# Second layer of the last six groups as seven block products, growth with 40 weight columns, decays turned ahead of minus x

## The chip, the cores and the metric

One core of one Trainium2 chip. The metric is device time in microseconds (us) of one execution of the whole program, the median of several runs; lower is better. The engines are TensorE (PE in the profile; its weight loads are listed apart as PEld), VectorE (DVE), ScalarE (ACT), GpSimd (POOL) and SyncE (SP), which issues most of the DMAs.

## What is computed

A recurrent attention layer, then a feed-forward layer on its output, all in float32:

```python
# r, k, v, w, a, b: (B=4, H=8, S=768, D=40); state: (B, H, D, D), zero at first
for t in range(S):
    y[t]  = einsum('bhd,bhde->bhe', r[t], state)
    Sa    = einsum('bhde,bhe->bhd', state, a[t])
    state = state * w[t][:, :, None, :] - outer(Sa, b[t]) + outer(v[t], k[t])
x = y.transpose(0, 2, 1, 3).reshape(3072, 320)
out = relu(x @ w_in) ** 2 @ w_out        # w_in: 320 x 2048, w_out: 2048 x 320
```

## The kernel before, in words

**Chunks and groups.** The sequence is cut into chunks of 128 tokens: 6 chunks of each of 4 batches, 24 in all, in the order chunk 0 of all batches, chunk 1 of all batches, and so on. Within a chunk the recurrence becomes matrix products and the solution of a triangular system. Two chunks that follow each other make a group (12 groups), the unit of the feed-forward layer.

**A chunk's work** is a chain (`chain`, lines 632 to 717) with a stop after each stage: right side `x_` from state and A, two products with the inverse T (`times_t`, giving `minus_x`), transposes of minus x (line 671), the products with `rT` masked to RX, then `y_`, and *growth*: the products that add to the state (lines 688 to 692), for each of 8 heads k by v and b by minus x. Growth exists for chunks 0 to 19, since the last chunk of a batch leaves no state behind. Its outputs lie two heads to a column of partitions, the even head at partition 0, the odd one at 64; a head has 40 columns, but weights were loaded 64 wide, 24 of them zero.

**Ahead of the chain** of the next chunk stand its turned inputs: `turn_rv` (transposes of r and v, copied by ACT at lines 560, 561), `make_rv` (RV), `turn_k` (transposes of k, DVE line 548), `turn_down` (line 582: transposes of the decays, whose result stays in PSUM), `scale_kb` (DVE line 588 reads that result), `make_a`, `turn_state` (line 598). `early` does the first part of chunks far ahead (scans of w, N) and is spent by slot 14. GpSimd solves the triangular systems (lines 478, 480), unit by unit of up to 4 chunks, and `inverses` loads the solved T (line 507).

**Order.** An opening, written out word by word, takes chunks 0 to 6. Then slot i (`sorted_slot`) finishes chunk i and turns chunk i + 1; its calls are the order of the instructions on each engine. `tick` after each step issues stores that were put off.

**The feed-forward layer** (`Ffn`). The first layer works by quads: 4 of the 16 blocks of 128 hidden features for a group's 256 tokens (`thirds` and `whole`), through two banks of PSUM (`ps_f`; in the tail, `ps_w`), ReLU by ACT (line 762) into `hidden`, squared by DVE (line 769). `hidden` holds six quads of 256 tokens, a ring. The second layer works by quarters (`make_quarter`): for one chunk, 4 matmuls whose weights are 128 hidden features by 128 tokens and whose moving side is 320 columns of `w_out`; four quarters fill a bank of `ps_f`, ACT copies it (line 790) and SP stores it. A slot begins two quarters (with `turn_rv` between them) and ends with two more; it makes two quads between. The group g has its quads in slots 2g + 3 and 2g + 4; its second layer begins at the end of slot 2g + 4. After slot 23 `rest` goes on with a quad and up to four quarters a turn (the tail).

Each float32 matmul of this kernel is two records in the profile, with a weight load each; a transpose is one.

Of the kernel before, what the change touches and what calls it, by code (L numbers as in the profile page):

```python
# [11 lines left out]
Alu = mybir.AluOpType  # L12
# [5 lines left out]
def kernel(  # L18
# [22 lines left out]
    nc = tc.nc  # L41
    ctx.enter_context(tc.manual_schedule())
    B, H, S, D = r.shape
# [42 lines left out]
    def mm(o, l_, r_, start):  # L86
        nc.tensor.matmul(o, l_, r_, start=start, stop=True, skip_group_check=True)  # L87
# [518 lines left out]
    def rest(i, g):  # L606
        begin(i, g)
        yield
        yield
        turn_k(i, g)  # L610
        yield
        make_a(i, g)
        yield
        turn_rv(i, g)
        yield
        make_rv(i, g)
        yield
        turn_down(i, g)
        yield
        scale_kb(i, g)  # L620
        yield
        yield
# [9 lines left out]
    def chain(i, g):  # L632
# [55 lines left out]
        if c < NCH - 1:  # L688
            grown = psum(ps_w)[:, :NP * D].rearrange("p (q d) -> p q d", q=NP)
            for l_, r_ in ((k_, v_), (b_, xn)):  # L690
                for h in range(H):
                    mm(grown[h % 2 * DP:(h % 2 + 1) * DP, h // 2], l_[:, h, :], r_[:, h, :D], l_ is k_ and h < 2)
        n = i % GB
        if n == 0:
            tokens[i // GB] = new("tokens", [128, NP, GB * C], 2)
# [1 line left out]
        nc.vector.tensor_tensor(t_, y_, g["up"][:, :, :C], Alu.mult)  # L697
        if c < NCH - 1:
            for e in range(2):
                rows = slice(e * DP, (e + 1) * DP)  # L700
                nc.vector.tensor_tensor(st[rows, :, e, :D], grown[rows], st[rows, :, e, :D], Alu.add)
            ended[bb] = new(f"end{bb}", [128, NP], 1)
            nc.scalar.copy(ended[bb], g["up"][:, :, C])
# [20 lines left out]
    class Ffn:  # L724
# [47 lines left out]

        def make_quarter(self):
            n, p = divmod(self.quarter, NQ)
            k = (n // GB) * NQ + p
            if n >= len(order) or self.squared <= k or left():
                return False
            if p == 0:
                self.out = psum(ps_f)[:, :DM]
            cols = slice((n % GB) * C, (n % GB + 1) * C)  # L780
            h_ = hidden[:, self.place(k)].rearrange("p e (f t) -> p e f t", f=2)
            for e in range(2):
                for m_ in range(2):
                    f = p * QF + 2 * m_ + e
                    mm(self.out, h_[:, e, m_, cols], w_out[:, f], p == 0 and e == 0 and m_ == 0)
            self.quarter += 1
            if p == NQ - 1:
                bb, c = order[n]
                o_ = new("o", [128, DM], 1)
                nc.scalar.copy(o_, self.out)  # L790
                at = bb * S + c * C
                store(out[at:at + C, :], o_, 6 if opening[0] else 2)
            return True

        def rest(self):
            self.tail = True
            last = len(order) * NQ
            while self.quarter < last:
                flush()
                self.thirds()  # L800
                self.whole()
                for _ in range(NQ):
                    self.make_quarter()
                self.square()


    second = Ffn()

# [175 lines left out]
    def sorted_slot(i, g, ch):  # L984
# [21 lines left out]
        fetch_next(j + 1, "r")  # L1006
        step(second.make_quarter)
        step(on(ch), of(decay_state))
        step(of(make_rv), second.thirds)
        step(on(ch), on(one))  # L1010
        if fine:
# [1 line left out]
        step(second.whole)  # L1013
        step(on(ch))
        step(on(one), of(turn_k))
        step(on(one), on(ch), of(turn_down))
        step(on(ch), of(scale_kb))
        if fine:
            join()
        step(on(ch), of(make_a), second.thirds, on(one))  # L1020
        fetch_next(j + 1, "v")
        step(of(turn_state), second.square, second.whole, on(two))
        if not early_join and not fine:
            join()
        run(ch)
# [54 lines left out]
```

## Time and profile before

| | |
|---|---|
| median of 3 runs | 950.41 us |
| the three runs | 949.51, 963.28, 950.41 us |
| span of the profiled execution | 949.3 us |
| mean granted TensorE clock | 0.958 |
| matmuls `ps_f<-w_out,hid` (second layer) | 768 records, 436 ns mean |
| matmuls `ps_f<-tokens,w_in` (first layer) | 672 records, 387 ns mean |
| growth, `ps_w<-in_v,in_k` and `ps_w<-minus_x,in_b` | 320 records each, 229 and 230 ns mean |

The profile is of one execution. Its page gives busy time by engine; tables by stretch give the same for parts of the span, with the granted clock; groups put together instructions of one line, engine and pair of tiles (`out<-in`), with count, busy time, mean length, and the idle time ahead of them with what ended it. The timeline shows runs of equal instructions: start, length, engine, line, count. Shown lengths of matmuls overlap, so that the distance from one start to the next says what one costs.

### The profile page before, as it was taken

The numbers are of one execution on the slowest core, as the hardware profiler recorded it, in microseconds if no ns is written. First come the engines' busy times: TensorE is split into PE (matmuls) and PEld (weight loads), VectorE is DVE, ScalarE is ACT, GpSimd is POOL, SyncE is SP. The second block draws the span as 40 slices with busy tenths as digits, with TensorE's granted clock in tenths as the row PEclk, the third lists the DMA queues.
The fourth block names the chain that finished last, engine by engine and source line by source line (L and its number), as shares of the span: only waits on it lengthen the run. The fifth ranks groups of instructions, "written<-read, shape, count | busy, mean of one in ns | idle before, by whom it ended". The sixth has DMA issues, their size and how long they took to land.

```text
span 949.3 us, 22557 instructions
## 1 busy us (share of the span) xinstructions
PE 896.9 (94%) x9116; PEld 719.2 (76%) x9116; DVE 462.1 (49%) x1131; ACT 284.8 (30%) x735; POOL 509.4 (54%) x935
## 2 busy tenths in 40 slices
PE   6578989879999999999999999999999999999998
PEld 4365656758787887888887888888888877887775
DVE  5927548788863355652664455544334331331110
ACT  3033334534532342342342232222221222222111
POOL 4568246064008786318999959999858870000000
PEclk9768988589999999999999999999999999999999
DMA  9788779856868477896846765604484154210000
GB/s 112 124 160 150 163 127 189 193 127 136 173 104 170 85 139 140 168 173 119 137 78 104 122 173 100 121 13 82 91 168 77 24 108 80 44 30 10 12 14 15
DMA packets 253266, 103.37 MB, mean 109 GB/s; under 512 B 234154, under 2 KB 240298, under 8 KB 252010
## 3 DMA queue, kind: packets, MB, share of 16 engines
q1 hardware_dynamic: 244709, 83.00, 49.2%
q0 software_dynamic: 3760, 17.10, 7.5%
q10 hardware_dynamic: 4693, 1.83, 0.9%
q8 instruction: 72, 1.18, 0.6%
q14 instruction: 32, 0.26, 0.1%
HBM read 69.00 MB, written 30.92 MB: 105 GB/s over the span
## 4 chain that ended last, share of the span: by engine, by line
PE 82%; DVE 6%; DMA 3%; ACT 3%; issue 2%; POOL 1%; SPq 1%; ACTq 0%; DVEq 0%; POOLq 0%
PE ps_f L87 40%; PE ps_w L87 17%; PE ps_c L87 14%; PE ps_w L331 5%; PE ps_f L264 2%; PE ps_c L671 2%; PE ps_c L598 1%; PE ps_w L582 1%; SPq L513 1%; DMA kept_q<-N 1%; DMA in_r<-in_r_dram 1%; DMA half_n<-kept_q 1%; ACT N L401 1%; DVE decay L381 1%; DVE decay L380 1%
## 5 line engine op out<-in xcount | busy, mean ns | idle before, releaser
L478 POOL TENSOR_TENSOR half_p<-half_n,half_t 128x462 f32<-128x462 f32 (+39 forms) x406 | 221.9, 547 | 74.3 <-DMA half_n<-kept_q 23.4
L480 POOL TENSOR_TENSOR half_t<-half_t,half_p 128x462 f32<-128x462 f32 (+39 forms) x406 | 237.7, 585 | 31.8
L87 PE MATMUL ps_f<-w_out,hid 128*128 128x320 f32 x768 | 218.4, 436 | 0.0
L87 PEld LDWEIGHTS ps_f<-w_out,hid 128*128 128x128 f32 x768 | 142.1, 190 | 54.0 <-issue 0.2
L87 PE MATMUL ps_f<-tokens,w_in 128*128 128x256 f32 x672 | 156.7, 387 | 0.0
L87 PEld LDWEIGHTS ps_f<-tokens,w_in 128*128 128x128 f32 x672 | 125.8, 192 | 18.7 <-issue 1.9
L769 DVE TENSOR_TENSOR hid<-hid 128x512 f32<-128x512 f32 x96 | 78.2, 853 | 50.6 <-ACT hid L762 50.2
L762 ACT ACTIVATE hid<-ps_f 128x512 f32<-128x512 f32 x84 | 49.5, 595 | 77.2 <-PE ps_f L87 77.1
L451 POOL DMA_DIRECT2D half_n<-kept_q x18 | 9.4, 526 | 88.4 <-DMA kept_m<-N 43.1
L372 DVE TENSOR_TENSOR_SCAN decay<-ps_w,ones 128x64 f32<-128x64 f32 x88 | 23.7, 270 | 67.0 <-PE ps_w L331 66.9
L697 DVE TENSOR_TENSOR tokens<-ps_c,dec 128x512 f32<-128x512 f32 x24 | 16.6, 691 | 79.6 <-PE ps_c L87 77.5
L347 DVE TENSOR_TENSOR RX<-ps_w,upper 128x512 f32<-128x512 f32 x48 | 30.8, 684 | 47.6 <-PE ps_w L87 47.4
L264 PE MATMUL ps_f<-ident 128*128 128x512 f32 (+3 forms) x108 | 49.8, 595 | 0.0
L347 DVE TENSOR_TENSOR RV<-ps_w,upper 128x512 f32<-128x512 f32 x48 | 30.9, 684 | 38.5 <-PE ps_w L87 38.2
L398 ACT COPY N<-ps_w 128x256 f32<-128x256 f32 x48 | 17.7, 368 | 94.4 <-PE ps_w L87 69.5
L87 PE MATMUL ps_f<-tokens,w_third 64*128 64x256 f32 x336 | 45.5, 381 | 0.1
L548 DVE TENSOR_TENSOR kvT<-ps_w,dec 128x512 f32<-128x512 f32 x24 | 16.4, 683 | 59.4 <-ACT minus_x L658 35.4
L87 PEld LDWEIGHTS ps_c<-xr,T 64*64 64x64 f32 x768 | 28.9, 143 | 20.7 <-issue 14.5
L570 DVE TENSOR_TENSOR f<-end,dec 128x4 f32<-128x4 f32 x20 | 7.5, 374 | 72.6 <-DMA dec<-kept_e 72.6
L331 PE MATMUL ps_w<-ident,in_ab 128*128 128x128 f32 x184 | 28.1, 298 | 11.9 <-DVE RV L347 10.0
L87 PE MATMUL ps_c<-xr,T 64*64 64x40 f32 x768 | 34.9, 237 | 3.8 <-ACT xr L647 2.6
L560 ACT COPY rT<-ps_w 128x512 f32<-128x512 f32 x24 | 14.0, 585 | 80.5 <-PE ps_w L331 80.4
(151 smaller groups left out, 1450.6 us busy)
## 6 DMA issues: line engine op xcount, KB each, us to landing
dec<-kept_e SPq DMA_DIRECT2D x22, 633.8 KB
kept_e<-decay SPq DMA_DIRECT2D x19, 633.8 KB
in_w<-in_w_dram SPq DMA_DIRECT2D x24, 160.0 KB
in_b<-in_b_dram SPq DMA_DIRECT2D x24, 160.0 KB
in_ab<-in_a_dram SPq DMA_DIRECT2D x24, 160.0 KB
in_r<-in_r_dram SPq DMA_DIRECT2D x24, 160.0 KB
in_v<-in_v_dram SPq DMA_DIRECT2D x24, 160.0 KB
out_dram<-o SPq DMA_DIRECT2D x24, 160.0 KB
```

Source lines behind the costliest of these rows:

```text
L87: nc.tensor.matmul(o, l_, r_, start=start, stop=True, skip_group_check=True)
L264: nc.tensor.matmul(fill_bank[:, :n * 128], ident, ident.unsqueeze(1).to_broadcast([128, n, 128]), start=True, stop=True, skip_group_check= ...
L331: nc.tensor.transpose(p_[:, q * 128:(q + 1) * 128], pair(x_, q), ident)
L347: nc.vector.tensor_tensor(t_, p_, over4(upper), Alu.mult)
L372: nc.vector.tensor_tensor_scan(up[:, q, MID + 1:C + 1], wT[:, q, MID:], ones, 1.0, Alu.mult, Alu.mult)
L398: nc.scalar.copy(plain, p_[:, ::2].rearrange("s h (f t) -> s f h t", f=2))
L478: eng.tensor_tensor(p_, part[:, at:at + m_].unsqueeze(1).to_broadcast([128, n, m_]), t3[:, :n, s:s + 1].to_broadcast([128, n, m_]), Alu.mult)
L480: eng.tensor_tensor(t3[:, :n, s + 1:], t3[:, :n, s + 1:], p_, Alu.subtract)
L671: nc.tensor.transpose(p_[:, q * 128:(q + 1) * 128], pair(xn, q), ident)
L697: nc.vector.tensor_tensor(t_, y_, g["up"][:, :, :C], Alu.mult)
L762: nc.scalar.activation(h_, p_.rearrange("p f t -> p (f t)"), Act.Relu)
L769: nc.vector.tensor_tensor(h_, h_, h_, Alu.mult)
```

## The change

The second layer of the groups 6 to 11 (`SEVEN = 6`) is no longer 32 matmuls of 320 columns but a 2 x 2 block product (two chunks by two halves of the hidden features, times two halves of the features by two halves of 160 output columns) in seven block products (Strassen's, in Winograd's form). Each of the seven has 8 matmuls of 128 x 128 weights and 160 moving columns. Sums ahead of and behind them are made by DVE:

- once, in slots 15 and 16 (`sum_weights`): three sums of blocks of `w_out` in tiles that are free by then, and one in place
- for each group, four sums of 128 x 1024 elements over the squared hidden features, in place
- for each group, eight sums of 128 x 160 elements, out of PSUM into two output tiles, and two ACT copies; both chunks are stored at the end

The pieces take the place of quarters, one for one; a group has eight places and seven pieces, so the eighth does nothing. The first piece, P4, needs all four quads of the group squared (in the last group P1 goes first, which needs two).

```diff
-                    mm(grown[h % 2 * DP:(h % 2 + 1) * DP, h // 2], l_[:, h, :], r_[:, h, :D], l_ is k_ and h < 2)
+                    mm(grown[h % 2 * DP:h % 2 * DP + D, h // 2], l_[:, h, :D], r_[:, h, :D], l_ is k_ and h < 2)
...
-                rows = slice(e * DP, (e + 1) * DP)
+                rows = slice(e * DP, e * DP + D)
                 nc.vector.tensor_tensor(st[rows, :, e, :D], grown[rows], st[rows, :, e, :D], Alu.add)
...
         def make_quarter(self):
             n, p = divmod(self.quarter, NQ)
+            if n < len(order) and n // GB >= SEVEN:
+                return self.make_piece(n // GB, n % GB * NQ + p)
...
+        def make_piece(self, g, at):
+            names = "P1 P4 P2 P7 P6 P5 P3" if g == len(order) // GB - 1 else "P4 P1 P2 P7 P6 P5 P3"
+            if at == 7:
+                self.quarter += 1
+                return True
+            name = names.split()[at]
+            if self.squared <= g * NQ + (1 if name == "P1" else 3):
+                return False
...
+            half, chunk = {"P1": (0, 0), "P2": (1, 0), "P4": (1, 1), "P7": (0, 1), "P6": (0, 0), "P5": (1, 1), "P3": (1, 0)}[name]
+            part = {"P1": 0, "P2": 2, "P4": 1, "P7": 0, "P6": 0, "P5": 1, "P3": 2}[name]
+            if at in (0, 3, 4):
+                self.bank = psum(ps_f)
...
+            for n in range(NF // 2):
+                k, e, m_ = n // 4, n // 2 % 2, n % 2
+                mm(ps[part], x_[:, n], seven[name][k * QF + 2 * m_ + e], at in (0, 3, 4) and n == 0)
...
+            a = lambda i, j: block(j, i)
...
+            if at == 1:
+                plus(a(1, 1), a(1, 0), a(1, 1))
+                less(a(1, 0), a(0, 0), a(1, 0))
+                less(a(0, 0), a(1, 1), a(0, 0))
+            if at == 2:
+                nc.scalar.copy(hi0, ps[0])
+                nc.scalar.copy(lo1, ps[1])
+                plus(lo0, ps[2], hi0)
+                less(a(0, 1), a(0, 1), a(0, 0))
+            if at == 3:
+                plus(hi1, ps[0], hi0)
+            if at == 6:
+                plus(hi0, ps[2], hi0)
+                plus(hi1, ps[0], hi1)
+                plus(hi0, ps[0], hi0)
+                less(lo1, hi1, lo1)
+                plus(hi0, ps[1], hi0)
+                plus(hi1, ps[1], hi1)
+                for n, o_ in enumerate(self.ends):
...
+                    store(out[row:row + C, :], o_, 2)
...
         step(on(ch), of(decay_state))
+        if i == 2 * SEVEN + 3:
+            sum_weights(0)
+        if i == 2 * SEVEN + 4:
+            sum_weights(3)
...
         step(on(one), of(turn_k))
-        step(on(one), on(ch), of(turn_down))
+        if i == 2 * SEVEN + 3:
+            sum_weights(1)
+        step(of(turn_down))
+        step(on(one), on(ch))
...
         step(of(turn_state), second.square, second.whole, on(two))
+        if i == 2 * SEVEN + 3:
+            sum_weights(2)
```

## The prediction on record

> **What bounds the kernel now.** I read the page first, then a table of stretches, then the groups by form, then the timeline of a late slot and of the end. The page:
>
> ```profile
> span 949.3 us, 22557 instructions
> ...
> PE 896.9 (94%) x9116; PEld 719.2 (76%) x9116; DVE 462.1 (49%) x1131; ACT 284.8 (30%) x735; POOL 509.4 (54%) x935
> ```
>
> A share of 94% over everything says little of a stage, so the stretches:
>
> ```profile
> core 0: us, PE busy (x) PEld busy (x) DVE busy (x) ACT busy (x) POOL busy (x), PEclk, DMA share, GB/s
> 0.00:100.00 100.00, 69.68 (x586) 50.52 (x587) 63.18 (x218) 29.40 (x80) 63.72 (x184) 0.81 0.84 138
> ...
> 330.00:545.00 215.00, 213.76 (x2537) 178.59 (x2536) 110.81 (x280) 73.11 (x202) 157.09 (x238) 1.00 0.75 131
> 545.00:640.00 95.00, 95.00 (x1009) 79.87 (x1008) 47.72 (x97) 25.87 (x67) 79.22 (x93) 1.00 0.51 103
> 640.00:735.00 95.00, 95.00 (x971) 77.59 (x970) 37.63 (x60) 21.88 (x51) 77.41 (x119) 1.00 0.55 104
> 735.00:830.00 95.00, 95.00 (x939) 77.41 (x939) 28.75 (x50) 23.70 (x54) 38.75 (x70) 1.00 0.32 63
> ```
>
> From 330 us on TensorE matmul is busy all the time at granted clock 1.00. All of the new second layer lies behind 640 us, where DVE has over half of its time free. So there the sum is one of matmul time, and other engines count only if they make TensorE wait.
>
> **The second layer.** How far apart matmuls start is what counts, since their shown durations overlap. Rows of the timeline (start, length, engine, line, instruction, count):
>
> ```profile
> 746.99 0.97 PEld L87 LDWEIGHTS ps_c<-rT,sd 128*128 128x128 f32 x8
> 747.10 1.06 PE L87 MATMUL ps_c<-rT,sd 128*128 128x128 f32 x8
> ...
> 751.43 3.62 PE L87 MATMUL ps_f<-tokens,w_in 128*128 128x256 f32 x16
> ...
> 932.53 13.08 PE L87 MATMUL ps_f<-w_out,hid 128*128 128x320 f32 x48
> ```
>
> and the groups by form (count, busy us, mean ns):
>
> ```profile
> L87 PE MATMUL ps_f<-w_out,hid 128*128 128x320 f32 x768 | 218.4, 436 | 0.0
> L87 PE MATMUL ps_f<-tokens,w_in 128*128 128x256 f32 x672 | 156.7, 387 | 0.0
> ...
> L87 PE MATMUL ps_c<-rT,sd 128*128 128x128 f32 x160 | 21.2, 276 | 0.0
> ...
> L87 PEld LDWEIGHTS ps_f<-w_out,hid 128*128 128x128 f32 x768 | 142.1, 190 | 54.0 <-issue 0.2
> ```
>
> 24 chunks by 16 products of 320 columns give 384 matmuls and 768 records, so each matmul is two records with a load each. Taking one duration off a run and dividing by the steps: 320 columns start every (13.08-0.44)/47 = 0.269 us, 256 every (3.62-0.39)/15 = 0.215, 128 every (1.06-0.28)/7 = 0.112. That is 0.84 ns a column within a few ns, also at 128 columns, where each matmul again has its own load of 128 columns (the row of PEld, as many as matmuls). A 160-column matmul is not in the trace; bounds from the neighbours are 0.112 and 0.215, and the straight line between them at 160 gives 0.138, the 320-column rate 0.135. I take 0.136.
>
> One group of two chunks now has 64 records, 64 x 0.269 = 17.2 us. The seven products are 7 x 8 matmuls of 160 columns, 112 records, 112 x 0.136 = 15.2 us. Six groups: **-11.9 us**. (One eighth of the columns is saved; the loads go from 64 to 112.)
>
> A rule that speaks against this stands in the Trainium skill, "TensorE: Matmul & The Clock Gate", The mechanism: a weight load runs beside matmuls in flight only if it goes to another group of rows. All loads here take all 128 rows; by that rule's letter 48 more loads of 0.112 us a group, 5.4, stand against 2.0 saved, +20 us over six groups instead of -11.9. The rows above disagree (269 ns from start to start with a 190 ns load for each). What is left of it is the first rival.
>
> **What the sums wait for.** DVE rows, with PSUM or SBUF sources, and the order of the work at the end of a slot:
>
> ```profile
> 756.77 0.61 PE L87 MATMUL ps_w<-in_v,in_k 128*64 128x40 f32 x16
> ...
> 756.99 0.69 DVE L697 TENSOR_TENSOR tokens<-ps_c,dec 128x512 f32<-128x512 f32 x1 [3.60 <-PE ps_c L87]
> ...
> 757.21 0.64 PE L87 MATMUL ps_w<-minus_x,in_b 128*64 128x40 f32 x16
> ...
> 757.68 0.75 PE L87 MATMUL ps_c<-state,dec 128*64 128x80 f32 x16
> ...
> 757.90 0.66 DVE L701 TENSOR_TENSOR state<-ps_w,state 64x160 f32<-64x160 f32 x2 [0.22 <-PE ps_w L87]
> ...
> 758.59 1.75 DVE L769 TENSOR_TENSOR hid<-hid 128x512 f32<-128x512 f32 x2
> ...
> 759.27 6.73 PE L87 MATMUL ps_f<-w_out,hid 128*128 128x320 f32 x24
> ```
>
> 512 elements take 0.69 us, 160 take 0.33, so an element is about 1.03 ns on 0.16 us: a block sum of 1024 is 1.22 us, 1.6 where GpSimd runs beside it (the 1.75 for two), and a weight sum of 1280 is 1.5 to 1.9. P4 comes first and needs the last square, which ends at 760.34. Its first six matmuls need only what was squared earlier or the first half, and at 759.27 they last 6 x 0.272 = 1.63 us, to 760.90; with growth 0.27 shorter still 0.3 us behind the square. The block sums start when P4 ends; the second, which P7 needs, is done 3.2 us later, and P1, P2 and the transposes of r and v lie between, 5.2 us. So **0** there, with 0.3 us of cover at P4; if DVE were late by 1 us, each of six groups would lose 0.7. In all the sums add 4 x 1.6 + 8 x 0.33 = 9 us of DVE in a group's two slots; of the 95 us from 640 on, some three slots, DVE has 57 free.
>
> Three things are not covered. The weight sums are made once, in slot 15: the second (1.9 us) goes between kT and the scaling of k and b, whose PSUM bank the second product of A takes over: **+1.1**. The others fall where DVE waits for a transfer or a product. Then the empty eighth piece: now a quarter lies between the transposes of r, v and the first product of T, and covers ACT's two copies.
>
> ```profile
> 765.84 0.60 PE L331 MATMUL ps_w<-ident,in_r 128*128 128x128 f32 x4
> ...
> 766.27 0.60 PE L331 MATMUL ps_w<-ident,in_v 128*128 128x128 f32 x4
> ...
> 766.47 0.59 ACT L560 COPY rT<-ps_w 128x512 f32<-128x512 f32 x1 [6.60 <-PE ps_w L331]
> ...
> 766.71 2.32 PE L87 MATMUL ps_f<-w_out,hid 128*128 128x320 f32 x8
> ...
> 766.96 0.59 ACT L561 COPY kvT<-ps_w 128x512 f32<-128x512 f32 x1
> ...
> 768.96 0.54 PEld L87 LDWEIGHTS ps_c<-xr,T 64*64 64x64 f32 x16 [0.44 <-issue]
> ...
> 769.55 1.16 PE L87 MATMUL ps_w<-rT,kvT 40*128 40x128 f32 x16
> ```
>
> kvT is there 1.71 us after the transposes begin. Without the quarter the product of T runs from 0.87 to 1.46, and rT,kvT would wait 0.3: in slots 18, 20 and 22 **+0.9**. Third, the end:
>
> ```profile
> 933.36 0.69 DVE L769 TENSOR_TENSOR hid<-hid 128x512 f32<-128x512 f32 x1 [1.03 <-ACT hid L762]
> ...
> 945.69 0.43 ACT L790 COPY o<-ps_f 128x320 f32<-128x320 f32 x1 [8.19 <-PE ps_f L87]
> ```
>
> After the last matmul stands one copy of 0.43 and a store to 949.3. Now come six sums of 0.33, 1.98, and two stores of 160 KB, the first one sum earlier: +1.55, and 0.15 for the second store, **+1.7**. In the last group P1 goes ahead of P4, so P7 follows P2 directly: two block sums, 2 x 1.22 + 0.1, against P2's 2.18: **+0.4**. P4 there needs the square that ends at 934.05, 1.5 us after its start at 932.53: its seventh matmul comes at 1.6; no wait.
>
> **Growth.** The rows at 756.77, 757.21 and 757.68 give 0.91 us for 32 records, 28 ns each with 64 weight columns and 40 moving. How a load depends on columns is seen only by a far row, 32 by 32:
>
> ```profile
> 542.45 0.69 PE L87 MATMUL ps_w<-blocks,spares 32*32 32x32 f32 x32
> 543.07 2.42 PE L87 MATMUL ps_f<-w_out,hid 128*128 128x320 f32 x8
> ```
>
> 0.62 us for 32 records, 19 ns. Bounds: nothing saved (the load goes by the group of 64 columns), or 32 x (28-19) = 0.29 us. A load of 40 is nearest to 32: I take 20 ns, 0.27 us a chunk. The 13 chunks 7 to 19 grow in the stretches where TensorE is full: **-3.5**; of the seven before 330 us, where it is not (69.68 busy in the first 100), I count **-0.5** (0 to 1.9). The Trainium skill, "TensorE: Matmul & The Clock Gate", LDWEIGHTS, says that a load's time is its columns over 1.2, whatever its rows; that is 53 ns for 64 and 33 for 40, an estimate of 20 ns for each pair of column groups, 0.32 us a chunk, 0.6 us more over 13.
>
> **Decays ahead of minus x.**
>
> ```profile
> 745.49 0.66 PE L331 MATMUL ps_w<-ident,in_k 128*128 128x128 f32 x4
> 745.63 0.60 ACT L658 COPY minus_x<-ps_c 64x160 f32<-64x160 f32 x2
> ...
> 745.98 0.84 PE L671 MATMUL ps_c<-ident,minus_x 128*128 128x128 f32 x4
> ...
> 746.66 0.60 PE L582 MATMUL ps_w<-ident,dec 128*128 128x128 f32 x4
> ```
>
> The four transposes of minus x take 0.68 from start to next start, those of in_r above 0.43: 0.24 us is a wait for ACT's second copy, at 746.23. The decays' 0.44 fills it. It falls in slots 15 to 22 (before, an early step's transposes stand there, and hide it): 8 x 0.24 = **-1.9**. The consumer moves too: minus x's transposes (0.44) and xnT's copy (0.59, as kvT's, which is of one size with it) take 1.1 us with what lies between, and the state product (8 x 0.112) ends 1.3 us after the transposes begin, so the copy stays covered by 0.2. No queue other than TensorE's is passed, and the added tick only delays stores that nobody waits for.
>
> **The sum.** -11.9 - 3.5 - 0.5 - 1.9 + 1.1 + 0.9 + 1.7 + 0.4 = -13.7. Against the execution's own span 949.3 that is 935.6; the fastest run is 949.51, so 0.2 lies around the span, and the median, 950.41, stands 1.1 above it. On the median I forecast **936.7 us**. All of it rests on TensorE staying full.
>
> **Rivals.**
> 1. Slower: loads come out from behind the shorter matmul. A load's row is 190 ns; if the next one cannot begin before the last has ended, a 160-column record takes 190, not 136. The point from which it decides is 17.2/112 = 154 ns. Price: 112 x 0.190 = 21.3 us a group, +4.1, six times 24.4; with the other terms -1.8, 973.0. For it: the load is longer than the matmul that hides it, as nowhere in the second layer now. Against: the state product, whose records start every 112 ns with loads as wide. 4%.
> 2. DVE makes TensorE wait: a late square at P4, a PSUM bank not yet summed at the next first layer, in each group. It takes 14/6 = 2.3 us a group to eat the gain: about 950. For it: margins of 0.3 us. Against: DVE's free half. 8%.
> 3. Growth gains nothing, since 40 columns sit in a group of 64: 940.7. 9%.
> 4. More: growth pays in all 20 chunks at 0.29 (-5.8), and the turned decays in all 16 slots (-3.8), the waits above vanish but the end: 949.3 - 11.9 - 5.8 - 3.8 + 1.7 = 929.5, on the median 930.6. 8%.
> 5. GpSimd, whose solving does not move with TensorE, becomes the bound.
>
> ```profile
> 690.73 1.28 SPq L507 DMA_DIRECT2D T<-kept_t  x2
> ...
> 707.25 0.66 PE L87 MATMUL ps_c<-xr,T 64*64 64x40 f32 x16
> ```
>
> The solved T of chunk 18 is asked for at 690.73 and used 16.5 us later; TensorE will be some 4 us ahead there. If GpSimd loses 10 us beside DVE's sums, TensorE waits a few: 941. 2%.
>
> **How the numbers follow.** The forecast has 69%, its own range 931 to 943. Range **929 to 945**: it takes in 3, 4 in part and 5, and leaves out 1 and most of 2. Within 2% of before (what a measurement of this kernel can just tell from no change) is 931.4 to 969.4. Faster by more: 4 and the forecast's low edge, 0.10. Slower: 1, 0.04. Within: 0.86.
>
> **What would show it.** Products starting every 0.136 us, blocks of 16 in 2.2 (if 0.15 or more, the first term fails); growth pairs of blocks in 0.64; minus x's transposes in 0.44 behind the decays'; slots shorter by about 1.5 us; no TensorE wait on DVE in the slots; the last matmul some 5.2 us ahead of the end. Waits of TensorE for DVE above 1 us a slot would make the prediction wrong.

## The result, and the profile after

The changed kernel takes 944.9 us (median of 19 runs, 942.24 to 952.6) against 950.82 (19 runs) of the kernel before: a ratio of 0.9937 [0.9918, 0.9957]. A ratio, with its 95% interval in brackets, is taken from the fast runs of both kernels and a median from all runs, so that the two can differ by 2 to 3 us. The gain is 5.9 us where 13.7 were forecast; the time lies at the upper edge of the range. The profiled execution has a span of 943.2 us against 949.3.

The page of the changed kernel: its span, the busy times (us, share, instructions), and the chain that ended last, by engine and then by line.

```profile
span 943.2 us, 23218 instructions
...
PE 883.6 (94%) x9404; PEld 738.8 (78%) x9404; DVE 518.8 (55%) x1209; ACT 283.0 (30%) x735; POOL 525.1 (56%) x935
...
PE 47%; POOL 25%; DVE 11%; DMA 8%; issue 4%; ACT 3%; SPq 2%; ACTq 0%; DVEq 0%; POOLq 0%
PE ps_f L87 21%; POOL half_t L480 13%; POOL half_p L478 12%; PE ps_w L87 11%; PE ps_c L87 8%; PE ps_w L331 3%; DMA half_n<-kept_d 2%; PE ps_f L264 2%; DMA in_r<-in_r_dram 1%; DMA T<-kept_t 1%; SPq L513 1%; DVE half_t L480 1%; DVE half_t L478 1%; DVE decay L381 1%; DMA dec<-kept_e 1%
```

TensorE is 13.3 us less busy (896.9 before), nearly the forecast. But the span gave back only 6.1 of it, and the chain, which went over TensorE for 82% of its length before (GpSimd 1%), now takes a quarter of its length on GpSimd. That piece ends in the store and the load of T (start, length):

```profile
693.76 5.14 DMA kept_t<-half_t
698.92 0.60 SPq L507
699.56 8.85 DMA T<-kept_t
```

So TensorE has stood still somewhere. The table of stretches shows where:

```profile
core 0: us, PE busy (x) PEld busy (x) DVE busy (x) ACT busy (x) POOL busy (x), PEclk, DMA share, GB/s
697.00:703.00 6.00, 6.00 (x48) 5.94 (x46) 0.65 (x3) 0.22 (x1) 1.44 (x5) 1.00 1.01 231
703.00:709.00 6.00, 0.64 (x11) 0.49 (x10) 0.83 (x4) 0.86 (x2) 0.91 (x4) 0.79 0.82 148
709.00:715.00 6.00, 6.00 (x57) 4.95 (x56) 0.00 (x0) 1.15 (x4) 4.98 (x14) 0.64 0.55 126
```

From 703 to 709 TensorE does nothing for over 5 us, and behind that the granted clock is 0.64 for 6 us. The timeline of the same place, slot 18 (start, length; in brackets the idle time ahead and what ended it):

```profile
693.76 0.60 POOL L487 DMA_DIRECT2D kept_t<-half_t  x1 [0.30 <-POOL half_t L480]
...
694.44 1.95 POOL L451 DMA_DIRECT2D half_n<-kept_d  x4
...
698.92 1.42 SPq L507 DMA_DIRECT2D T<-kept_t  x2
...
702.58 0.60 PE L331 MATMUL ps_w<-ident,in_v 128*128 128x128 f32 x4
...
707.85 0.29 POOL L478 TENSOR_TENSOR half_p<-half_n,half_t 128x63 f32<-128x63 f32 x1 [7.29 <-DMA half_n<-kept_d]
...
708.54 1.08 PE L87 MATMUL ps_c<-xr,T 64*64 64x40 f32 x16 [5.36 <-DMA T<-kept_t]
...
709.55 2.08 PE L87 MATMUL ps_w<-rT,kvT 40*128 40x128 f32 x16
...
711.42 1.92 PE L87 MATMUL ps_f<-tokens,w_third 64*128 64x256 f32 x8
```

GpSimd has solved the unit of chunks 18 to 21 and stores T at 693.76; the store lands, SP asks for the T of chunk 18 at 698.92, beside the 1536 KB of the next unit's system that GpSimd has been asking for since 694.44 (four issues of 384 KB; the expectations below call it 768 KB). T lands at 708.41 and is used at 708.54. TensorE has waited **5.36 us**. The steps behind it then run at half speed: they begin 1.01, 1.87 and 1.85 us apart, where 0.59, 0.99 and 0.96 are usual: another **2.19 us**. Together 7.55; 943.2 - 7.55 is 935.65, and the forecast for the span was 935.6. That they meet so closely is partly luck: chunk 6 reached `y_` (DVE line 697) 1.2 us later in this execution than in the one before (323.27 against 322.11), where 0.5 less was forecast, and the rest of the change brought some 1.6 us more than its terms. In the kernel before, at the same place:

```profile
685.57 0.60 POOL L487 DMA_DIRECT2D kept_t<-half_t  x1 [0.30 <-POOL half_t L480]
...
704.57 0.60 PE L331 MATMUL ps_w<-ident,in_v 128*128 128x128 f32 x4
...
705.01 2.32 PE L87 MATMUL ps_f<-w_out,hid 128*128 128x320 f32 x8
```

The store was 8.2 us earlier, TensorE 2.0 us later, and a quarter of the second layer stood ahead of the product of T.

The terms of the sum, in rows of the changed kernel's timeline: products, growth, decays ahead of minus x, and the end.

```profile
667.41 4.51 PE L87 MATMUL ps_f<-w_out,hid 128*128 128x160 f32 x32
...
748.98 0.60 PE L582 MATMUL ps_w<-ident,dec 128*128 128x128 f32 x4
...
749.42 0.60 PE L671 MATMUL ps_c<-ident,minus_x 128*128 128x128 f32 x4
...
749.86 1.06 PE L87 MATMUL ps_c<-rT,sd 128*128 128x128 f32 x8
...
759.53 0.47 PE L87 MATMUL ps_w<-in_v,in_k 128*40 128x40 f32 x16
...
759.83 0.48 PE L87 MATMUL ps_w<-minus_x,in_b 128*40 128x40 f32 x16
...
760.14 0.75 PE L87 MATMUL ps_c<-state,dec 128*64 128x80 f32 x16
...
938.44 0.33 DVE L825 TENSOR_TENSOR o<-ps_f,o 128x160 f32<-128x160 f32 x1 [6.19 <-PE ps_f L87]
938.68 0.32 DVE L825 TENSOR_TENSOR in_w<-ps_f,in_w 128x160 f32<-128x160 f32 x1
```

A 160-column record starts every (4.51 - 0.30)/31 = 0.136 us, with 0.30 the group's mean length. The loads beside them still show 190 ns, so that rival 1, by which a record would take as long as its load, is out. Growth takes 0.61 us from 759.53 to 760.14, against 0.91. Minus x's transposes take 0.44 behind the decays'.

### The profile page after: what moved, and what is told of

The parts are those of the page before. It is cut to its first block, busy times and chain, and to the rows that moved or that the text cites. A ratio compares the mean times of both kernels' runs of the same rounds, so it can differ in the third digit from the quotient of the medians.

```text
span 943.2 us, 23218 instructions
## 1 busy us (share of the span) xinstructions
PE 883.6 (94%) x9404; PEld 738.8 (78%) x9404; DVE 518.8 (55%) x1209; ACT 283.0 (30%) x735; POOL 525.1 (56%) x935
## 3 DMA queue, kind: packets, MB, share of 16 engines
q10 hardware_dynamic: 4693, 1.83, 0.9%
## 4 chain that ended last, share of the span: by engine, by line
PE 47%; POOL 25%; DVE 11%; DMA 8%; issue 4%; ACT 3%; SPq 2%; ACTq 0%; DVEq 0%; POOLq 0%
PE ps_f L87 21%; POOL half_t L480 13%; POOL half_p L478 12%; PE ps_w L87 11%; PE ps_c L87 8%; PE ps_w L331 3%; DMA half_n<-kept_d 2%; PE ps_f L264 2%; DMA in_r<-in_r_dram 1%; DMA T<-kept_t 1%; SPq L513 1%; DVE half_t L480 1%; DVE half_t L478 1%; DVE decay L381 1%; DMA dec<-kept_e 1%
## 5 line engine op out<-in xcount | busy, mean ns | idle before, releaser
L478 POOL TENSOR_TENSOR half_p<-half_n,half_t 128x462 f32<-128x462 f32 (+39 forms) x406 | 229.2, 565 | 75.7 <-DMA half_n<-kept_q 23.7
L480 POOL TENSOR_TENSOR half_t<-half_t,half_p 128x462 f32<-128x462 f32 (+39 forms) x406 | 245.7, 605 | 31.8
L87 PE MATMUL ps_f<-w_out,hid 128*128 128x320 f32 (+1 forms) x768 | 165.4, 368 | 0.0
L87 PEld LDWEIGHTS ps_f<-w_out,hid 128*128 128x128 f32 x768 | 123.2, 190 | 26.0
L769 DVE TENSOR_TENSOR hid<-hid 128x512 f32<-128x512 f32 x96 | 82.3, 899 | 10.3 <-ACT hid L762 9.9
L87 PE MATMUL ps_f<-tokens,w_third 64*128 64x256 f32 x336 | 47.6, 394 | 0.1
L347 DVE TENSOR_TENSOR RV<-ps_w,upper 128x512 f32<-128x512 f32 x48 | 30.9, 685 | 21.2 <-PE ps_w L87 20.9
L658 ACT COPY minus_x<-ps_c 64x160 f32<-64x160 f32 x96 | 27.5, 287 | 36.5 <-PE ps_c L87 32.6
L87 PE MATMUL ps_w<-rT,kvT 40*128 40x128 f32 x384 | 31.4, 308 | 5.4 <-ACT kvT L561 5.1
```

The lines of the kernel that those rows point to most:

```text
L347: nc.vector.tensor_tensor(t_, p_, over4(upper), Alu.mult)
L478: eng.tensor_tensor(p_, part[:, at:at + m_].unsqueeze(1).to_broadcast([128, n, m_]), t3[:, :n, s:s + 1].to_broadcast([128, n, m_]), Alu.mult)
L480: eng.tensor_tensor(t3[:, :n, s + 1:], t3[:, :n, s + 1:], p_, Alu.subtract)
L658: nc.scalar.copy(flipped(xn)[halves[half], flip, :, :, :D], by_pair(xs[halves[half ^ flip]]))
L769: nc.vector.tensor_tensor(h_, h_, h_, Alu.mult)
```

## The experiments

**The theory** after the result: the terms of TensorE hold; what is missing is the wait for T in slot 18. GpSimd finishes its unit late because DVE's sums with both operands in SBUF hold it up, and TensorE comes earlier; whatever TensorE gains ahead of slot 18 is lost there. **Rivals:** one of the two halves of the change brings less than it seems; the 1536 KB transfer beside T makes T late, not GpSimd; the loss belongs to the clock.

What the theory says of GpSimd is seen in the timeline, where a sum over weights (DVE, line 879) and the block sums of the first group (lines 825, 826) lie beside the solving (POOL, lines 478, 480):

```profile
621.09 1.10 POOL L478 TENSOR_TENSOR half_p<-half_n,half_t 128x528 f32<-128x528 f32 x1
...
621.56 1.98 DVE L879 TENSOR_TENSOR decay<-decay,w_out 128x1280 f32<-128x1280 f32 x1
...
622.27 2.35 POOL L480 TENSOR_TENSOR half_t<-half_t,half_p 128x528 f32<-128x528 f32 x1
...
669.63 3.62 DVE L826 TENSOR_TENSOR hid<-hid 128x1024 f32<-128x1024 f32 x2
...
670.38 1.78 POOL L480 TENSOR_TENSOR half_t<-half_t,half_p 128x375 f32<-128x375 f32 x1
```

The same instructions in the kernel before:

```profile
621.35 1.22 POOL L480 TENSOR_TENSOR half_t<-half_t,half_p 128x528 f32<-128x528 f32 x1
...
665.02 0.92 POOL L480 TENSOR_TENSOR half_t<-half_t,half_p 128x375 f32<-128x375 f32 x1
```

The GpSimd instruction beside a sum of 1280 elements is 1.13 us longer (2.35 for 1.22), the one beside a sum of 1024 0.86 us (1.78 for 0.92). The Trainium skill, "SBUF — State Buffer", SBUF: two separate sides, says that a DVE instruction with two SBUF inputs and a GpSimd instruction that reads SBUF take turns at a shared port, each holding it for a whole instruction; the rows agree, with 0.86 and 1.13 us as the price of one turn.

### The halves apart

**growth_turn_only**: growth and the turned decays alone.

```diff
-    SEVEN = 6
+    SEVEN = 12
```

> Second layer as before; growth with 40 columns and the turned decays alone. Theory (late T: DVE's SBUF sums hold GpSimd up by 8 us in the unit of chunks 18 to 21, so that TensorE, some 4 us ahead, waits 5.4 us for chunk 18's T and then runs 2.2 us slower): without the sums GpSimd stores that unit near 685 us as before, TensorE does not wait in slot 18, and 13 x 0.30 + 8 x 0.24 = 5.8 us come off: ratio 0.994, about 945. Rival (the gain of these two was lost in the opening, which ran 1.2 us longer in the profile of after): less than 4 us come off, ratio above 0.996.

945.57 us, 0.9912 [0.9874, 0.9949], against 951.32 before (25 runs): the medians are 5.7 apart, where the forecast had 5.9 for these two; the ratio makes it 8 us (5 to 12). GpSimd stores at 682.88, and T is not waited for. In this execution another wait shows, of 3.76 us in slot 9, and with the slow records behind it that slot takes 5.4 us longer than it should, so that the nearness of 5.7 to 5.9 is luck in part. The terms are seen better slot by slot: from one chunk's `y_` to the next it takes 0.30 us less than before up to chunks 11 to 14, and 0.54 less up to chunks 15 to 20. The wait in slot 9:

```profile
410.19 1.35 SPq L513 DMA_DIRECT2D blocks<-kept_t  x2
...
411.30 1.03 POOL L451 DMA_DIRECT2D half_n<-kept_d  x2 [24.81 <-DMA kept_d<-N]
...
419.11 0.91 ACT L522 ACTIVATE T<-blocks,which 128x256 f32<-128x256 f32 x2 [6.96 <-DMA blocks<-kept_t]
...
421.35 1.21 PE L671 MATMUL ps_c<-ident,minus_x 128*128 128x128 f32 x4 [3.76 <-ACT minus_x L658]
```

The load of the solved blocks of chunk 10 is asked for in two issues, the second (410.89) only 0.41 us ahead of GpSimd's 1536 KB; the blocks land 8 us later. In the kernel before the second issue went out 0.76 us ahead of that fetch, and the blocks were there 2.5 us after it. But in the changed kernel, 0.44 us ahead, they were there after 2.7 us, and in from_group_7, 0.43 us ahead, after 7.2, so the lead alone does not tell.

**products_only**: the products alone; growth 64 columns wide and the decays where they were.

```diff
-                    mm(grown[h % 2 * DP:h % 2 * DP + D, h // 2], l_[:, h, :D], r_[:, h, :D], l_ is k_ and h < 2)
+                    mm(grown[h % 2 * DP:(h % 2 + 1) * DP, h // 2], l_[:, h, :], r_[:, h, :D], l_ is k_ and h < 2)
...
-        step(of(turn_down))
-        step(on(one), on(ch))
+        step(on(one), on(ch), of(turn_down))
```

> Seven products as in after; growth with 64 columns and the decays turned where they were. Theory (late T): GpSimd's store stays near 694 us, TensorE comes to slot 18 without its lead of 4 us and waits some 2 to 3.5 us instead of 5.4; 11.9 less 3.2 for the uncovered places, less 3 for the wait and up to 2 for the clock: 4 to 6 us come off, ratio 0.994 to 0.996. Rival (the wait does not depend on how far TensorE is ahead, but on the transfer): 5.4 of wait as in after.

947.23 us, 0.9955 [0.9921, 0.9989]: 4.1 gained, of 7.8 forecast. TensorE waits 2.50 us for T (used at 707.70, stored at 692.97), the clock stays full after it, and 1.83 us for k of chunk 19 behind that; 4.1 + 4.3 is 8.4. So each half is worth about what its terms say, less its waits. But 5.7 and 4.1 are 9.8, and the two together bring 5.9. The intervals are too wide to show from the times alone that the halves do not add; the traces show why they would not. T is used 14.7 and 14.8 us after GpSimd's store here and in the changed kernel, but TensorE asks for it at 705.20 here and at 703.18 there: a TensorE that is quicker ahead of slot 18 only waits longer in it. That neither half is at fault speaks against the first rival.

**from_group_7**: the products from the next group on, so that group 6 has no block sums and the sums over weights come two slots later.

```diff
-    SEVEN = 6
+    SEVEN = 7
```

> SEVEN = 7: five groups in products instead of six; the sums begin one group (two slots) later. Theory (late T): only two weight sums, some 2 us, fall on GpSimd before it stores the unit of chunk 18, near 688 us; T lands near 702, before TensorE needs it: no wait in slot 18, 9.9 + 3.9 + 1.9 less 3.1 = 12.6 us come off, ratio 0.987, about 938, faster than after with less work saved. Rival (the products themselves cost TensorE more than their matmuls show): one group less saves less, ratio nearer to 1 than after's 0.994.

940.63 us (4 runs), 0.9868 [0.9803, 0.9932]: 4.3 us less than the changed kernel's median, though it has one group less of products. Only one of DVE's sums, over weights, lies ahead of the store here; GpSimd stores at 684.35, and T is not waited for. In this execution a wait of 3.0 us stands in slot 9.

### Which transfer is late

**last_take_later**: the 1536 KB of the last unit are asked for by SP, behind T.

```diff
+        if i == 17:
+            take(unit, [nc.sync])
...
-        while unit < len(units) and all(m_ in done for m_ in range(len(order)) if unit_of[m_] == unit):
+        while unit < len(units) and (unit < 10 or i > 16) and all(m_ in done for m_ in range(len(order)) if unit_of[m_] == unit):
...
-            take(unit, own)
+            if unit < 10:
+                take(unit, own)
```

> As after, but the 768 KB that GpSimd fetches for its last unit are issued by SyncE behind the load of chunk 18's T, not by GpSimd ahead of it. Theory in its first form (T lands late, 9 us after its issue, since it shares the DMA engines with this transfer): T issued near 699 lands near 703, TensorE waits under 1 us, and some 6 to 7 us more come off than in after: ratio 0.986 to 0.988. Rival (the load of T is slow by itself, in small pieces): T still lands near 708, the wait stays 4 to 5 us, and the ratio is after's.

946.68 us, 0.9948 [0.9917, 0.9979]. In the profiled execution a wait of 5.93 us in slot 9 made TensorE so late that T was not waited for in slot 18, so the time says nothing of the theory. The trace does: by the events of its semaphore T landed at 704.21, 9.5 us after the store (694.71). TensorE used it at 711.98, and then waited 2.1 us for k of chunk 19. The pair was tried again below with slot 9 free.

**blocks_by_act**: to free slot 9, the blocks of chunk 10 on ScalarE's queue.

```diff
-        joining = n.pop("joining") if early_join else inverses(j, n) if more else iter(())
+        joining = n.pop("joining") if early_join else inverses(j, n, nc.scalar if j == 10 else nc.sync) if more else iter(())
```

> As after, with one load moved: the blocks of chunk 10 are issued on ScalarE's queue at the start of slot 9, not on SyncE's behind the stores of chunk 17. Theory (a second late transfer: in some executions these blocks are issued 0.4 us ahead of GpSimd's 768 KB and then take 8 us instead of 2.5, and TensorE waits 3 to 6 us for them in slot 9): the blocks land before 412 us in every execution, no wait in slot 9, runs of one kernel lie closer together than the 10 to 15 us seen; the wait for chunk 18's T stays (5 us, and 2 of slow clock), the median falls by 0 to 3 us below after's. Rival (the wait in slot 9 has to do with the narrower growth, not with that transfer): it stays in some executions.

946.87 us, 0.9954 [0.9926, 0.9982]: no remedy. ScalarE was itself held between the two issues (405.27 and 409.75), and TensorE waited 3.6 us in slot 9 for ScalarE's copy. T was used at 708.30, after a wait of 2.10.

**from_group_7_blocks**: both edits, `SEVEN = 7` and the blocks by ScalarE.

> SEVEN = 7 and the blocks of chunk 10 on ScalarE's queue. Theory: neither the wait in slot 9 nor the one in slot 18; against from_group_7 its 3 us in slot 9 and the clock's 2 come off in those executions that had them: median 936 to 939, ratio 0.983 to 0.988, runs close together. Rival: as from_group_7, 0.987 with the same spread.

944.09 us, 0.9904 [0.9869, 0.994]: the products from group 7, without a wait for T (stored at 690.82), but 7.8 us of waiting for ScalarE in slot 9. The remedy costs more than the wait.

**T18_by_gpsimd**: blocks_by_act, and T of chunk 18 asked for by GpSimd ahead of the 1536 KB.

```diff
+        joining = n.pop("joining") if early_join else inverses(j, n, {10: nc.scalar, 18: nc.gpsimd}.get(j, nc.sync)) if more else iter(())
...
+        while unit < len(units) and (unit < 10 or i > 16) and all(m_ in done for m_ in range(len(order)) if unit_of[m_] == unit):
```

> As blocks_by_act, and chunk 18's T is loaded on GpSimd's queue, right behind the store of its unit and ahead of the 768 KB for the last unit; SyncE is no longer blocked by it. Theory (late T, from the slowed solving and from the transfer beside it): GpSimd still stores near 694, T lands near 703 instead of 708.5, TensorE waits under 1.5 us, SyncE fetches k of chunk 19 in time; 5 to 7 us come off after, ratio to before 0.985 to 0.988, near 937. Rival (T's landing is bound by its small pieces, whoever issues it): wait of 4 to 5 us as in after, ratio 0.992 to 0.994.

950.71 us, 0.9973 [0.994, 1.0007], a miss. T is not waited for, but k of chunk 19 now is, by 3.95 us (at 721.64), and slow records follow. GpSimd stored late (697.24), since the wait for ScalarE in slot 9 is here too, and T landed 10.2 us after that store. So T is quicker ahead of the big transfer, and k of chunk 19 is late behind it.

**blocks_early**: the blocks of chunk 10 asked for at the end of slot 8, as those of later chunks are.

```diff
-            if soon(j) and j > B:
+            if soon(j) and j > B or j == 10:
```

> As after (SEVEN = 6), but the blocks of chunk 10 are asked for at the end of slot 8, on SyncE ahead of chunk 17's stores, so that they cannot meet the 768 KB that GpSimd fetches once those stores have landed. Theory: blocks land some 10 us before use, no wait in slot 9 in any execution, runs lie closer together; the wait of 5 us for chunk 18's T and the slow clock behind it stay: 943 to 945, ratio 0.991 to 0.993. Rival (slot 9's wait comes from elsewhere): it stays.

945.23 us, 0.9917 [0.9884, 0.9951]. Slot 9 is free: the blocks are asked for at 405.66, the 1536 KB at 414.41. The wait for T is 5.72 us, to 707.03, with slow records behind it. That what slot 9 gives is lost again in slot 18 fits the median, which is near that of the changed kernel; the intervals are too wide to show it.

**before_blocks_early**: the same edit in the kernel before.

> The kernel before with that load moved and nothing else. Theory: before meets the slot 9 wait seldom, since its blocks are issued 0.8 us ahead of the 768 KB: within 2 us of before, ratio 0.998 to 1.001, with fewer runs above 953. Rival (before met it as often): 3 us or more come off.

949.68 us, 0.9986 [0.996, 1.0011]: no clear difference, so the wait in slot 9 costs the kernel before little at most. One run of 12 is above 953 us here, against 9 of 28, as expected if some executions of the kernel before have that wait; no trace shows one.

**last_take_later_early**: blocks_early and last_take_later together (one run).

> blocks_early with the 768 KB for the last unit issued by SyncE behind T (as last_take_later, where TensorE came too late to slot 18 to show T's landing). Theory in its second form (two parts of T's 15 us: 4 to 5 us for the store to land, then 9 us for T, slow through the 768 KB beside it): T lands 8 to 10 us after the store's issue, near 702, TensorE waits 0 to 2 us for it, and k of chunk 19 is late instead. Rival (T takes 9 us by its small pieces): it lands near 707 again.

Its timeline, where SP now asks for the 1536 KB after T:

```profile
691.75 0.60 POOL L487 DMA_DIRECT2D kept_t<-half_t  x1 [0.30 <-POOL half_t L480]
...
698.00 1.28 SPq L507 DMA_DIRECT2D T<-kept_t  x2
...
700.32 1.84 SPq L451 DMA_DIRECT2D half_n<-kept_d  x4
...
702.27 0.66 PE L87 MATMUL ps_c<-xr,T 64*64 64x40 f32 x16 [2.05 <-DMA T<-kept_t]
...
702.87 1.16 PE L87 MATMUL ps_w<-rT,kvT 40*128 40x128 f32 x16
...
719.47 1.12 PE L331 MATMUL ps_w<-ident,in_k 128*128 128x128 f32 x4 [9.74 <-DMA in_k<-in_k_dram]
```

T lands 10.5 us after the store, not 14.5 to 15.2, and 3.6 us after the last of its two issues (698.64); in the changed kernel it took 9.0 from the last issue (699.56). So the big transfer costs T some 4 to 5 us: the second rival has a part. It is no part of what the change added, since the kernel before has the same transfer ahead of T, and T landed 14.0 us after the store there. But k then waits 9.74 us behind the big transfer, and the run takes 947.33. No order of these transfers that was tried spares TensorE a wait.

### GpSimd's lateness made and taken away

**no_weight_sums**: blocks_by_act without the four sums over `w_out` (the weights of the products are left unsummed; one run).

```diff
     def sum_weights(n):
+        if n < 4:
+            return
```

> As blocks_by_act, without the four sums over w_out (the products take what lies in those tiles, so the last six groups' output is not the reference's): DVE keeps the sums over the hidden features. Theory (each DVE sum of two SBUF operands holds the GpSimd instruction beside it, 1.13 us for 1280 elements, 0.86 for 1024): GpSimd stores the unit of chunk 18 about 4.5 us earlier against its start than in after (139.3 us from the fetch to the store there, 131.5 before), that is some 135 us; the wait for T in slot 18 falls from 5.4 to 0 to 2. Rival (GpSimd is slowed by the faster transfers or by the products' reads, not by DVE's sums): its 139 us stay.

The store comes at 686.99, 140.0 us after the unit's system was fetched, against 145.1 in blocks_by_act: 5.1 us less. T is not waited for; 938.42 us. That is 7.3 us less than the profiled run of blocks_by_act (945.71), of which 1.5 come ahead of the `y_` of chunk 6. The block sums of group 6 are left here, and their price shows alone: the four GpSimd instructions beside them are 0.71 to 0.87 us longer than the same ones in the kernel before, 3.3 us in all. Some 2 us more, here as in blocks_by_act, go by between the fetch and the start of the solving. (The lengths that the expectation gives were counted from another start; from the fetch they are 143.1 for the changed kernel and 134.9 for the kernel before.)

**no_weight_sums_early**: the same on blocks_early (one run).

> blocks_early without the four sums over w_out (the last six groups' output is not the reference's). Theory: GpSimd's time from fetch to store falls by 4.5 to 5 us against blocks_early, T lands 15 us behind the store near 702 to 703, the wait of 5.7 in slot 18 falls to 0 to 2 and the clock stays full: the profile 6 to 8 us shorter than blocks_early's 941.7 but for the opening. Rival (the block sums alone hold GpSimd up as much): wait over 4.

Half a miss. The solving is 3.8 us shorter (138.7 against 142.5), but GpSimd began 2.1 us later in this execution, so that the store came only 1.7 us earlier. T comes at 705.06, and TensorE still waits 4.04 us; 943.78 us. So the sums over weights are half of what GpSimd loses, and the block sums of the first group, which stand beside the same unit, are most of the rest (3.3 us in no_weight_sums). The wait is what the rival has (over 4), but not by its reason: the block sums alone hold GpSimd up about half as much as all the sums.

**gpsimd_late**: growth_turn_only with the early blocks and no products at all, and 15 idle instructions on GpSimd ahead of the unit's store.

```diff
+        if u == 9:
+            for _ in range(15):
+                eng.memset(new("half_p", [128, 528], 1), 0.0)
```

> blocks_early's load and growth_turn_only's second layer (as before: no products, no DVE sums), with 15 GpSimd memsets of 528 elements, some 8 us, between the solving of chunks 18 to 21 and its store. Theory (T of chunk 18 lands 14.5 to 15 us after the issue of that store, whatever TensorE does, and TensorE waits for it): the store goes from 683 to 691, T lands near 706, TensorE, at 703 there, waits some 3 us in slot 18; the products are not needed for the loss. Rival (the wait comes with the products, through the banks or the queues): no wait in slot 18.

957.92 us, 1.0053 [1.002, 1.0085]: the gain of growth and decays is turned into a loss. The store came later than expected (699.50, not 691): the 15 instructions made the solving 7.0 us longer than in growth_turn_only, and the unit was fetched 9.6 us later in this execution.

```profile
699.50 0.60 POOL L490 DMA_DIRECT2D kept_t<-half_t  x1
...
713.93 1.08 PE L87 MATMUL ps_c<-xr,T 64*64 64x40 f32 x16 [6.00 <-DMA T<-kept_t]
...
714.93 2.08 PE L87 MATMUL ps_w<-rT,kvT 40*128 40x128 f32 x16
```

The same wait with the same slow records, without one product: a late store is enough. From the `y_` of chunk 17 to that of chunk 18 it takes 40.5 us, where the kernel before takes 30.9. This kernel without the 15 instructions was not run.

**from_group_7_early**: `SEVEN = 7` with the early blocks.

> As blocks_early with SEVEN = 7. Theory: no wait in slot 9, none in slot 18, so that all that is left of the sum shows: five groups 9.9, growth 3.9, turned decays 1.9, less 1.0 for the weight sums, 0.5 for the empty piece and 1.5 at the end: 12.7 off, 937 to 939, ratio 0.985 to 0.988, faster than blocks_early by 4 to 7 us. Rival (the gain of the products is not there even without waits): ratio above 0.990.

940.64 us (6 runs), 0.9887 [0.9831, 0.9944].

```profile
686.87 0.60 POOL L487 DMA_DIRECT2D kept_t<-half_t  x1 [0.30 <-POOL half_t L480]
...
701.87 0.66 PE L87 MATMUL ps_c<-xr,T 64*64 64x40 f32 x16
...
710.95 0.66 PE L331 MATMUL ps_w<-ident,in_k 128*128 128x128 f32 x4 [1.63 <-DMA in_k<-in_k_dram]
```

No wait for T, and 1.63 us for k of chunk 19 instead; DVE is waited for 1.0 us there. The median lies a little above the 937 to 939 expected, and the interval reaches past the rival's 0.990. T was only just in time: by the events of its semaphore it landed at 701.44, 0.43 us ahead of its use. The executions side by side (us; solving is from the fetch of the unit to its store, the lag from the store to the product of T):

| kernel | store | solving | lag | wait for T |
|---|---|---|---|---|
| before | 685.57 | 134.9 | 21.7 | none |
| before_blocks_early | 688.00 | 135.5 | 21.3 | none |
| growth_turn_only | 682.88 | 136.0 | 22.8 | none |
| from_group_7 | 684.35 | 136.6 | 22.2 | none |
| from_group_7_early | 686.87 | 137.3 | 15.0 | none |
| no_weight_sums_early | 690.19 | 138.7 | 14.9 | 4.04 |
| from_group_7_blocks | 690.82 | 139.3 | 19.8 | none |
| no_weight_sums | 686.99 | 140.0 | 17.0 | none |
| products_only | 692.97 | 143.1 | 14.7 | 2.50 |
| after | 693.76 | 143.1 | 14.8 | 5.36 |
| blocks_early | 691.88 | 142.5 | 15.2 | 5.72 |
| gpsimd_late | 699.50 | 143.0 | 14.4 | 6.00 |
| filled_wait | 693.60 | 144.2 | 14.5 | 6.88 |
| blocks_by_act | 693.41 | 145.1 | 14.9 | 2.10 |

Wherever TensorE waits, T is used 14.4 to 15.2 us after GpSimd's store, whatever TensorE did. Where it does not wait, the events of T's semaphore put the landing at 13.8 to 15.1 us after the store (14.0 in the kernel before). Only the order of the transfers changed that: 9.5 to 10.4 us with T ahead of the big one.

### The clock

**filled_wait**: blocks_early, and 12 records of filling (5.2 us) put into slot 18 ahead of T, to keep TensorE busy.

```diff
+        if i == 18:
+            fill_in(24)
```

> As blocks_early, with six matmuls of 512 columns on the identity (5.2 us of work whose result nobody reads) where TensorE waits for chunk 18's T in slot 18. Theory (the idle time itself lowers the granted clock, 2.2 us lost behind the wait): the first product with T starts where it did, near 708.5 less the shift, but the product, rT,kvT and the thirds behind it take 0.59, 0.99 and 0.96 us again instead of 1.01, 1.87 and 1.85: 2 us faster than blocks_early. Rival (the product and what follows are slow for another reason, the transfer beside it): they stay slow, and no time is won.

945.91 us, 0.9939 [0.9911, 0.9968]: no gain on blocks_early. In the profiled execution TensorE came so early that it waited 6.88 us behind the filling all the same, and the clock fell to 0.50. Whether filling keeps the clock is not settled; that T comes at its own time (708.13) is. So the third rival, the clock, is left with what the rows of the changed kernel give it: 2.19 of the 7.55 us, behind the wait.

## Why the prediction was wrong

- **The products, -11.9:** right. 0.136 us a record makes 15.2 us for the 112 of a group.
- **Growth, -4.0, and turned decays, -1.9:** right behind the opening; 0.30 us a chunk (0.27 predicted) and 0.24 us a slot, as growth_turn_only shows slot by slot. The 0.5 us of the opening cannot be seen, since executions of one kind differ there by more: chunk 6 reached `y_` at 322.11 in the kernel before and at 323.99 in before_blocks_early.
- **Weight sums, +1.1:** right, 0.95: `dec,kvT` of slot 15 waits 0.56 us for DVE, and its block takes 1.84 us, not 0.89.
- **P4 and the other waits for DVE, 0:** right but for 0.38 us at the first group's P4, which takes 2.66 us from start to next start where the others take 2.28 (the two squares ahead of it took 2.64 us, where those of the next group took 1.29); P7 of the last group waits 0.40, as predicted.
- **The end, +1.7:** too much. Last matmul to end is 4.80 us against 3.66 in the kernel before, so +1.1: the six sums are 0.32 long but begin 0.23 apart.
- **The empty piece, +0.9:** its price was right (0.30 us each in slots 20 and 22: from the transposes of in_v to rT,kvT 1.33 us, where 0.44 and 0.59 make 1.03), its weighing was not. The quarter of 2.24 us that it removed from slot 18 had not only covered ACT's copies, but also kept TensorE from asking for T that early. Without it TensorE asks for T at 703.18, 4.1 us earlier than before (707.25), of which 2.0 are the gains ahead.
- **"All of it rests on TensorE staying full":** this is the step that failed, by **rival 5**, which had 2%. "Asked for at 690.73 and used 16.5 us later" read the time from issue to use as slack. Of it 8.9 us are the landing, beside the 1536 KB: the events of its semaphore put it at 699.59, so that the slack was 7.7 us. TensorE 4.1 us earlier and GpSimd 8.2 us later make 12.3, less that slack 4.6; T also landed 14.6 us after the store instead of 14.0, and was used 0.1 us behind its landing, which makes 5.3: measured 5.36. The price of rival 5 (941) also left out the 2.19 us at half clock.
- **DVE's sums** were costed in DVE's own time (9 us in a group's two slots, most of it free) and by TensorE's waits for them. That each of them holds GpSimd's instruction had no term. GpSimd's solving became 8.2 us longer with the sums over weights and group 6's blocks beside it; three kernels without these sums spread over 134.9 to 136.0 us, so that all but about 1 us of it is theirs.

What stays open: which transfer order would spare both T and k; how much of the spread between executions is the opening, where the same slot begins some microseconds earlier or later; what decides whether slow records follow a short wait; and what made the blocks of chunk 10 late with a lead of 0.43 us and not with 0.44.

## The better version

The products from group 7 on (from_group_7, from_group_7_early) had the lowest medians, 940.63 and 940.64 us, with ratios of 0.9868 [0.9803, 0.9932] and 0.9887 [0.9831, 0.9944]. Both beat the kernel before; against the changed kernel's 0.9937 [0.9918, 0.9957] the intervals overlap, so that the 4.3 us between the medians are likely and not certain. And T comes only just in time (0.43 us in from_group_7_early), so that a further gain ahead of slot 18 would be lost in it.

## What to carry to other kernels

When an engine off the path feeds the path once per unit, its slack is from landing to use, and every gain on the path and every sum that holds the feeder is taken from that slack; work that is moved away takes its cover along. Before DVE work is added beside a GpSimd solve, count the sums with both operands in SBUF as GpSimd's time too, and try the variant that starts the new scheme one unit later. Halves that gain well alone but do not add point at one shared arrival time.

## What the runs showed of the hardware that was not expected

- A DVE sum of two SBUF operands lengthens the GpSimd instruction beside it by 0.86 us (1024 elements) to 1.13 (1280); DVE pays too, 1.98 to 2.29 us for a sum of 1280, where the rate of the rows without GpSimd makes 0.16 + 1280 x 1.03 ns = 1.48.
- A small load beside a transfer of 1536 KB can land late: T (256 KB) 9.0 us after its last issue with the big transfer asked for ahead of it, 3.6 with it behind; the blocks of chunk 10 (128 KB) 7.2 to 8.2 us after theirs in three executions where it came 0.41 to 0.43 us ahead of the big one, 2.7 with 0.44 and 2.5 with 0.76.
- The clock after a wait: waits of 3.00 to 9.74 us were followed by records at half speed, waits of 2.05 and 2.50 us were not. But one of 2.10 us (blocks_by_act) was, with a delay:

```profile
708.30 0.66 PE L87 MATMUL ps_c<-xr,T 64*64 64x40 f32 x16 [2.10 <-DMA T<-kept_t]
...
708.89 1.16 PE L87 MATMUL ps_w<-rT,kvT 40*128 40x128 f32 x16
...
709.89 1.58 PE L87 MATMUL ps_f<-tokens,w_third 64*128 64x256 f32 x8
...
711.39 1.08 PE L87 MATMUL ps_c<-minus_x,N 64*64 64x40 f32 x16
...
712.40 6.01 PE L87 MATMUL ps_f<-tokens,w_in 128*128 128x256 f32 x16
...
718.34 0.66 PE L87 MATMUL ps_c<-xr,T 64*64 64x40 f32 x16
```

The first steps are at their usual distance (0.59), the next, 1.50 and 5.94 apart, are not (0.96 and about 3.7). The Trainium skill, "TensorE: Matmul & The Clock Gate", What's actually happening, puts the fall to half clock behind an idle window of about 3.4 us that runs freely; the waits of 3.60 us and more agree, and those of 3.00 (from_group_7) and 2.10 us do not.
- Two loads on ScalarE's queue held ScalarE itself: 4.5 us lay between their issues, and its copies waited.
